# First product of a four-expert mixture by seven half-size products, with sums of its weights made once and streamed

## The chip, the cores and the metric

The kernel runs on one core of one Trainium2 chip. The metric is the device time of one execution in microseconds (us); lower is better. All arithmetic is in float32.

## The reference

Two blocks follow each other. The first is a recurrence over 768 steps for 4 x 8 heads of width 40; the second is a mixture of four two-layer networks on the 3072 x 320 rows that the first one gives.

```python
# r, k, v, w, a, b: (B=4, H=8, S=768, D=40)
for t in range(S):
    y[:, :, t] = einsum('bhd,bhde->bhe', rt, state)
    Sa = einsum('bhde,bhe->bhd', state, at)
    state = state * wt[:, :, None, :] - einsum('bhd,bhe->bhde', Sa, bt) + einsum('bhd,bhe->bhde', vt, kt)
x = y.transpose(0, 2, 1, 3).reshape(3072, 320)
p = domain_probs / (domain_probs.sum(-1, keepdims=True) + 1e-9)
for e in range(4):                      # w1: (4, 320, 1024), w2: (4, 1024, 320)
    out += p[:, e:e + 1] * (maximum(x @ w1[e], 0) @ w2[e])
```

## The kernel before

**Units and chunks.** The sequence is cut into 12 chunks of 64 steps. A unit is one chunk of two batch entries (16 heads, 128 partitions of tokens), so there are 24 units; two units of one chunk make 256 rows for the mixture. `within` prepares a unit (decays, triangular scores), `substitute` inverts small triangles (on GpSimd from unit 2 on), `merge` joins the inverses, and `step` carries the state and ends with `Y`, the unit's result. For chunks from the third on, `step` moves `Y` into the transposed rows `xT` (320 feature rows in three groups of partitions, by 256 tokens) with twelve small DMAs on SyncE's queue (line 750).

**The mixture of a chunk** (`mixture_of_chunk`). For each of the four experts: two calls of `up_main`, each for half of the 1024 hidden columns, multiply `xT` by w1, 128 x 128 weights against 256 moving columns; the last 64 of the 320 features are done by `up_last` with four 64 x 64 tiles of the array. ScalarE applies the relu into `hs`. The second product (hidden rows times w2) is already done by seven half-size products instead of eight: `add_h` makes five sums of `hs` on VectorE (`a1`, `a7`, `a5`, `a2`, `a6`), `add_weights` made the sums of w2 once, and `down_1` and `down_2` multiply and let VectorE add the results, scaled by the gate, to the output tile `osb`. The results of matmuls of the mixture share three PSUM banks, tag `mm`, taken in turn; a bank is taken again only when the readers of its former content are done.

**Order.** The matmuls are kept in program order. A list `todo` holds the pieces of the mixture, and the main loop (line 1106) puts two of them into each of four gaps between the attention stages of a unit, so an expert takes two gaps and a chunk takes the eight gaps of two units. The second product of an expert is run in the gaps of the next expert. `lead` runs the 64 x 64 part of a piece ahead of it. After the last unit the remaining pieces run back to back.

**Weights.** w1 doesn't stay on the core. `load_piece` brings half an expert (512 KB and twice 64 KB) into one of two buffers for each use, and `used` starts the load of a later piece when a buffer comes free. All these loads, the loads of the inputs, the moves into `xT` and the stores of the output stand in one queue, SyncE's (SP), whose instructions are carried out in order. VectorE and ScalarE also work their queues in order, in an order that is fixed when the program is built.

Of the kernel before, what the change touches and what calls it, by code (L numbers as in the profile page):

```python
# [15 lines left out]
def kernel(  # L16
# [184 lines left out]

    def load(q, names):
        for x in names:
            q.n[x] = t = sb.tile([P, H, D], FP32, name=f"nat{x}", tag=f"nat{x}", bufs=2 if x in "WV" else 1)
            for i, bb in enumerate(q.b):
                nc.sync.dma_start(
                    out=t[i * L:(i + 1) * L], in_=srcs[x][bb, :, q.c * L:(q.c + 1) * L, :].rearrange("h t e -> t h e"),
                )
# [52 lines left out]

    w2_sb = [const.tile([P, NF, DM], FP32, name=f"w2_{e}") for e in range(E)]
    gate = const.tile([P, NC, B // 2, E], FP32, name="gate")
    minus_gate = const.tile([P, NC, B // 2, E], FP32, name="minus_gate")
# [10 lines left out]
    class Piece:  # L277
        pass

    n_pieces = 2 * E * (1 + NC)  # L280
    pieces = []

    in_sums = {k + 5 * x: k - 1 for x in range(3) for k in (1, 2, 3)}
# [1 line left out]
    def load_piece():  # L285

        k = len(pieces)
        e, x = k // 2 % E, k % 2
        if k in in_sums:
            t = sums[in_sums[k]]  # L290
        else:
            t = sb.tile([P, PIECE], FP32, name="w1p", tag="w1p", bufs=2)
        q = Piece()
        q.main = t[:, 0:2 * HF * P].rearrange("p (g c) -> p g c", g=2)
        q.last = t[:, 2 * HF * P:PIECE].rearrange("p (f c) -> p f c", c=P)
        cols = slice(x * HF * P, (x + 1) * HF * P)
        moves = [(q.main, moe_w1[e, 0:2 * P, cols].rearrange("(g p) c -> p g c", p=P))]
        for i in range(2):
            half_cols = slice((2 * x + i) * HF // 2 * P, (2 * x + i + 1) * HF // 2 * P)
            moves.append(  # L300
                (q.last[i * DT:(i + 1) * DT], moe_w1[e, 2 * P:DM, half_cols].rearrange("d (f c) -> d f c", c=P))
            )
        for to, src in moves:
            tc.keep_in_program_order(nc.sync.dma_start(out=to, in_=src))
        pieces.append(q)

    def used(n):

        while len(pieces) < n_pieces:
            k = len(pieces)  # L310
            if k in in_sums:
                before = k - 5 if k >= 5 else -1
            else:
                at = [x for x in range(k) if x not in in_sums]
                before = at[-2] if len(at) > 1 else -1
            if before >= n:
                break
            load_piece()

    def load_w2(e):  # L320
        tc.keep_in_program_order(nc.sync.dma_start(out=w2_sb[e][:], in_=moe_w2[e].rearrange("(f p) d -> p f d", p=P)))
# [84 lines left out]
    def within(q):  # L406
# [43 lines left out]
        yield  # L450

        pg = by(turn("pg", tok(Gv), q.u == 2)[:], 64)[:, :, 0:D]
        gp = sb.tile([P, H, D], FP32, name="gp")
        pin(nc.vector.tensor_tensor(out=gp[:], in0=pg, in1=n["W"][:], op=ALU.mult))
        pin(nc.vector.reciprocal(out=gp[:], in_=gp[:]))  # L455

# [314 lines left out]
    def up_main(k, xT, n, ph):  # L771

        w1 = pieces[k]
        h = sb.tile([P, HF, 2 * P], FP32, name="hs", tag="hs", bufs=3)
        for i in range(2):
            for f in range(HF // 2):
                for g in range(2):
# [29 lines left out]
    def mixture_of_unit(q):  # L807
# [3 lines left out]
        def ups(e):  # L811
# [6 lines left out]
            def piece():  # L818
                lead()
                hs[e] = [up_main(at + 2 * e, q.xT, P, ph[0])]  # L820
                hs[e].append(up_main(at + 2 * e + 1, q.xT, P, up_last(at + 2 * e + 1, q.xT, P)))
                used(at + 2 * e + 2)
                if q.u == 0 and e + 2 < E:
                    load_w2(e + 2)

            piece.lead = lead
# [32 lines left out]
    def add_weights(e):  # L859

        b = {(q, x): of_w2(e, q, x) for q in range(2) for x in range(2)}
        for to, x, y, op in (
# [6 lines left out]
            tc.keep_in_program_order(nc.vector.tensor_tensor(out=to, in0=x, in1=y, op=op))  # L869
            yield  # L870

    def mixture_of_chunk(qs, xT):

        hs, a_sums, osb = {}, {}, []
        at = 2 * E * (qs[0].c + 1)

        def ups(e, x):
            k, ph = at + 2 * e + x, []

            def lead():  # L880
                if not ph:
                    ph.append(up_last(k, xT, 2 * P))

            def piece():
                lead()
                hs[e, x] = up_main(k, xT, 2 * P, ph[0])
                used(k + 1)

            piece.lead = lead
            return piece  # L890

        def of_h(e, s, x):
            return hs[e, x][:, :, s * P:(s + 1) * P]

        def add_h(e):
            a = {(s, x): of_h(e, s, x) for s in range(2) for x in range(2)}
            for n, x, y, op in (
                (1, a[0, 0], a[1, 1], ALU.add), (7, a[0, 1], a[1, 1], ALU.subtract),
                (5, a[0, 0], a[0, 1], ALU.add), (2, a[1, 0], a[1, 1], ALU.add),
                (6, a[1, 0], a[0, 0], ALU.subtract),  # L900
            ):
                t = a_sums[e, n] = sb.tile([P, HF, P], FP32, name=f"a{n}")
                nc.vector.tensor_tensor(out=t[:], in0=x, in1=y, op=op)  # L903

        def products(name, *terms):
            p = ps.tile([P, len(terms) * HD], FP32, name=name, tag="mm", bufs=3)
            for n, (a, b) in enumerate(terms):
                for f in range(HF):
                    matmul(
                        out=p[:, n * HD:(n + 1) * HD], lhsT=a[:, f, :], rhs=b[:, f, :],  # L910
                        start=(f == 0), stop=(f == HF - 1),
                    )
            return p

        left, right, wide = slice(0, HD), slice(HD, DM), slice(0, DM)

        def down_1(e):
            p = products(
                "p431", (of_h(e, 1, 1), of_w2(e, 1, 0)), (of_h(e, 0, 0), of_w2(e, 0, 1)),
                (a_sums[e, 1], of_sums(e, 0)),  # L920
            )
            if e == 0:
                osb.extend(outputs() for _ in qs)

            for q, o in zip(qs, osb):
                add(o[:], p[:, wide], scale(q, e), e == 0)
            for q, o, cols in zip(qs, osb, (left, right)):
                add(o[:, cols], p[:, DM:DM + HD], scale(q, e))

        def down_2(e):  # L930
            p75 = products("p75", (a_sums[e, 7], of_sums(e, 2)), (a_sums[e, 5], of_w2(e, 1, 1)))
            p26 = products("p26", (a_sums[e, 2], of_w2(e, 0, 0)), (a_sums[e, 6], of_sums(e, 1)))
            for q, o, p, cols, n in ((qs[0], osb[0], p75, left, 1), (qs[1], osb[1], p26, right, 0)):
                add(o[:], p[:], scale(q, e))
                add(o[:, cols], p[:, n * HD:(n + 1) * HD], scale(q, e, minus=True))
            if e == E - 1:
                for q, o in zip(qs, osb):
                    store(q, o)

        def down_2_at_end(e):  # L940

            p75 = products("p75", (a_sums[e, 7], of_sums(e, 2)), (a_sums[e, 5], of_w2(e, 1, 1)))
            p2 = products("p2", (a_sums[e, 2], of_w2(e, 0, 0)))
            p6 = products("p6", (a_sums[e, 6], of_sums(e, 1)))
            add(osb[0][:], p75[:], scale(qs[0], e))
            add(osb[0][:, left], p75[:, right], scale(qs[0], e, minus=True))
            store(qs[0], osb[0])
            add(osb[1][:, left], p2[:], scale(qs[1], e))
            add(osb[1][:, right], p2[:], scale(qs[1], e, minus=True))
            store(qs[1], osb[1], left)  # L950
            add(osb[1][:, right], p6[:], scale(qs[1], e))
            store(qs[1], osb[1], right, nc.scalar)


        before = last[:]
        for e in range(E):
            todo.append(ups(e, 0))
            if before:
                todo.append(before[0])
                todo.append(ups(e, 1))  # L960
                todo.append(lambda e=e, then=before[1]: (then(), add_h(e)))
            else:
                todo.append(lambda e=e, then=ups(e, 1): (then(), add_h(e)))
            second = down_2_at_end if (qs[0].end and e == E - 1) else down_2
            before = [lambda e=e: down_1(e), lambda e=e, second=second: second(e)]
        last[:] = before


# [47 lines left out]
    ws = [within(units[u]) for u in range(3)]  # L1016
    norm = normalize()
    keep_warm(16)
    run(ws[0], 1)
    go(load_raw(units[1], "W"))  # L1020
    run(ws[0], 1)
# [16 lines left out]
    substitute(units[0], nc.vector, scores_of(0))  # L1038
    run(ws[0], 1)
    set_pick()  # L1040
    m, s = merge(units[0]), begin_step(0)
    run(m, 1)
    run(ws[0])
# [4 lines left out]
    load(units[2], "W")  # L1048
    for x in "VR":
        load_padded(units[2], x)  # L1050
    load_piece()
    load_piece()
    run(ws[1], 1)
    go(load_raw(units[2], "A"))
    load_w2(0)
    load_piece()
    load_piece()
    run(m)
    run(ws[1], 1)
    run(s, 3)  # L1060
# [16 lines left out]
            run(norm)  # L1077

    substitute(units[1], nc.vector, scores_of(1), during_second)
    m, s = merge(units[1]), begin_step(1)  # L1080
    run(m, 1)
    run(ws[2], 1)
# [23 lines left out]
    for u in range(1, NU):  # L1106
# [38 lines left out]
        if u == 1:  # L1145
            mixture_of_unit(q)
        elif q.bp:
            mixture_of_chunk(units[u - 1:u + 1], chunks_x[q.c])
        if not early:
            begin_later(len(later))  # L1150
            run(w, 1)
# [85 lines left out]
```

## Time and profile before

| | |
|---|---|
| device time, median of 3 runs | 1097.55 us (1096.2 to 1104.36) |
| profiled execution: its own time | 1096.91 us |
| profiled execution: span | 1095.2 us, mean TensorE clock 0.988 |
| busy: TensorE matmul / weight load | 1068.1 us / 959.0 us |
| busy: VectorE / ScalarE / GpSimd | 759.0 / 353.4 / 490.3 us |
| DMA | 122.19 MB, mean 112 GB/s |

A row of the profile gives line, engine, operation, "out<-in", shapes and count, then the busy time, the mean length of one, and the idle time before it with what ended it. Matmuls overlap, so that the mean length of one is longer than the distance to the next; a float32 matmul leaves two records. PE is TensorE, PEld its weight loads, DVE VectorE, ACT ScalarE, POOL GpSimd, SPq the queue of SyncE.

### The profile page before, as it was taken

How to read it: one execution, taken by the hardware profiler on the slowest of the kernel's cores; microseconds unless marked ns; L12 is line 12 of the kernel's file. 1: busy time of each engine (PE TensorE's matmuls, PEld its weight loads, DVE VectorE, ACT ScalarE, POOL GpSimd, SP SyncE). 2: the span in 40 equal slices, each digit the busy share in tenths (PEclk: the TensorE clock that was granted, in tenths of full speed). 3: DMA queues.
4: the chain of work that ended last, by engine and by line, in shares of the span. 5: the costliest groups of instructions: out<-in, count | busy, mean ns of one | idle time of the engine just before them, and what ended most of it. 6: DMA issues, size and time to landing. Idle time of an engine off the chain costs nothing.

```text
span 1095.2 us, 38536 instructions
## 1 busy us (share of the span) xinstructions
PE 1068.1 (98%) x16102; PEld 959.0 (88%) x16102; DVE 759.0 (69%) x1551; ACT 353.4 (32%) x956; POOL 490.3 (45%) x1274
## 2 busy tenths in 40 slices
PE   7798999999999999999999999999999999999998
PEld 6677788889998999999999999989999999998887
DVE  7676569887776777767768768767777676544343
ACT  2432444234223333333233242343333332221110
POOL 5206577763472562653643634735625536420000
PEclk8799999999999999999999999999999999999999
DMA  7876545434444463454454454444543532322320
GB/s 118 236 231 142 131 91 131 107 77 108 120 119 105 110 144 97 103 146 97 100 133 105 106 122 106 115 99 105 131 103 85 149 89 60 99 71 79 107 75 13
DMA packets 268869, 122.19 MB, mean 112 GB/s; under 512 B 213736, under 2 KB 242072, under 8 KB 268696
## 3 DMA queue, kind: packets, MB, share of 16 engines
q1 hardware_dynamic: 265416, 119.12, 43.4%
q8 instruction: 127, 2.08, 0.8%
q10 hardware_dynamic: 3280, 0.61, 0.4%
q14 instruction: 46, 0.38, 0.1%
HBM read 111.79 MB, written 3.93 MB: 106 GB/s over the span
## 4 chain that ended last, share of the span: by engine, by line
PE 92%; DVE 4%; ACT 1%; DMA 1%; issue 1%; SPq 0%; DVEq 0%; ACTq 0%
PE ph L76 39%; PE p L76 31%; PE pdy L76 3%; PE psat L76 2%; PE pxr L76 2%; PE po L76 2%; PE prn L76 2%; PE pfe L76 1%; PE pc L76 1%; PE pQ L76 1%; PE pev L76 1%; PE pg L79 1%; PE pY L76 1%; DVE Z L595 1%; PE pe L76 1%
## 5 line engine op out<-in xcount | busy, mean ns | idle before, releaser
L76 PE MATMUL ph<-xT,w1p 128*128 128x256 f32 (+3 forms) x3040 | 443.9, 375 | 3.7 <-issue 3.6
L76 PEld LDWEIGHTS ph<-xT,w1p 64*64 64x64 f32 (+1 forms) x3040 | 337.7, 162 | 59.3 <-issue 18.9
L598 POOL TENSOR_TENSOR Z<-Z 128x31 f32<-128x31 f32 (+7 forms) x704 | 254.8, 362 | 55.2
L903 DVE TENSOR_TENSOR a<-hs 128x512 f32<-128x512 f32 x220 | 153.3, 714 | 105.9 <-ACT hs L784 105.9
L784 ACT ACTIVATE hs<-ph 128x512 f32<-128x512 f32 (+1 forms) x208 | 117.1, 564 | 332.0 <-PE ph L76 331.7
L585 POOL TENSOR_TENSOR Z<-M,Z 128x62 f32<-128x62 f32 (+7 forms) x352 | 148.6, 422 | 99.0 <-DVE M L574 73.1
L76 PE MATMUL p<-sums,a 128*128 128x160 f32 x1056 | 164.9, 299 | 0.0
L76 PEld LDWEIGHTS p<-sums,a 128*128 128x128 f32 x1056 | 152.8, 190 | 2.2
L797 DVE SCALAR_TENSOR_TENSOR osb<-p,gate,osb 128x320 f32<-128x320 f32 (+1 forms) x243 | 108.0, 481 | 62.6 <-PE p L76 57.5
L555 POOL COPY below<-F 32x256 f32<-32x256 f32 x48 | 21.4, 446 | 232.2 <-ACT F L511 230.6
L76 PEld LDWEIGHTS p<-w,hs 128*128 128x128 f32 x704 | 98.6, 190 | 8.5 <-issue 7.3
L76 PE MATMUL p<-w,hs 128*128 128x160 f32 x704 | 104.9, 302 | 0.0
L76 PE MATMUL p<-w,a 128*128 128x160 f32 x704 | 102.8, 299 | 0.0
L76 PEld LDWEIGHTS p<-w,a 128*128 128x128 f32 x704 | 98.0, 190 | 0.0
L617 POOL COPY QT<-QTc 32x256 f32<-32x256 f32 x96 | 40.4, 421 | 81.9 <-DVE QTc L611 68.7
L706 ACT COPY RS<-pxr 64x256 f32<-64x256 f32 x88 | 32.2, 366 | 99.7 <-DVE SX L404 66.6
L540 ACT COPY EV<-pev 64x160 f32<-64x160 f32 x96 | 23.0, 286 | 91.6 <-PE pev L76 91.2
L455 DVE RECIPROCAL gp<-gp 128x320 f32<-128x320 f32 x24 | 51.6, 2151 | 0.7
L404 DVE COPY_PREDICATED VC<-mask_up,pc 128x256 f32<-128x256 int32 x48 | 18.7, 442 | 45.4 <-PE pc L76 45.3
L558 DVE STREAM_TRANSPOSE M<-blocks 128x1024 f32<-128x1024 f32 x24 | 47.2, 1969 | 2.9 <-ACT blocks L552 2.4
L511 ACT COPY F<-pfe 128x256 f32<-128x256 f32 x48 | 15.5, 376 | 80.9 <-PE pfe L76 79.3
L76 PE MATMUL pdy<-VC,k_tok 64*64 64x104 f32 (+1 forms) x768 | 38.2, 259 | 0.0
(149 smaller groups left out, 1343.9 us busy)
## 6 DMA issues: line engine op xcount, KB each, us to landing
w1p<-in_moe_w_dram SPq DMA_DIRECT2D x95, 512.0 KB
w1p<-in_moe_w_dram SPq DMA_DIRECT2D x190, 64.0 KB
w<-in_moe_w_dram SPq DMA_DIRECT2D x4, 1280.0 KB
sums<-in_moe_w_dram SPq DMA_DIRECT2D x9, 512.0 KB
natW<-in_w_dram SPq DMA_DIRECT2D x48, 80.0 KB
natB<-in_b_dram SPq DMA_DIRECT2D x48, 80.0 KB
natK<-in_k_dram SPq DMA_DIRECT2D x48, 80.0 KB
out_dram<-osb SPq DMA_DIRECT2D x46, 80.0 KB
```

The lines of the kernel that those rows point to most:

```text
L76: return stated(nc.tensor.matmul(**k))
L455: pin(nc.vector.reciprocal(out=gp[:], in_=gp[:]))
L540: nc.scalar.copy(out=of_slot(q.EV[half(p)], i ^ p)[:, :, 0:D], in_=pev[i][half(p)])
L555: tc.keep_in_program_order(nc.gpsimd.tensor_copy(out=q.below[quarter(i)], in_=q.F[quarter(i), :, 0:Q]))
L558: ins = nc.vector.transpose(out=M[:], in_=cols)
L585: ins = eng.tensor_tensor(out=Z[:, 1:3, 0:n, j + 1:Q], in0=M[:, j:j + 2, None, j + 1:Q].to_broadcast([P, 2, n, m]), in1=Z[:, here, 0:n, j: ...
L598: eng.tensor_tensor(out=z[:, 0], in0=z[:, 0], in1=z[:, x], op=ALU.add)
L617: ins = nc.gpsimd.tensor_copy(out=q.QT[quarter(i), :, quarter(i % 2)], in_=QTc[quarter(i)])
L706: nc.scalar.copy(out=RS[half(s), x ^ s::2], in_=prs[x][half(s)].rearrange("p (j i) t -> p j i t", i=2),)
L784: nc.scalar.activation(out=h[:, i * HF // 2:(i + 1) * HF // 2, 0:n], in_=ph[i][:], func=ACTF.Relu,)
L797: nc.vector.scalar_tensor_tensor(out=to, in0=p, scalar=sc, in1=to, op0=ALU.mult, op1=ALU.add)
L903: nc.vector.tensor_tensor(out=t[:], in0=x, in1=y, op=op)
```

## The change

For the chunks from the third on (`FIRST = 2`), `mixture_by_seven` takes the place of `mixture_of_chunk`. The product of 256 rows, 256 features and 1024 hidden columns is cut in two in each direction, and the four results are made of seven products of 128 rows x 128 features x 512 columns instead of eight. This needs four sums of the rows (`add_x`, on VectorE once a chunk), four sums of the quarters of w1, and seven results that are joined: one product (`u`) is left standing in its PSUM bank and two more are added onto it there, ScalarE copies it out three times, and VectorE adds the other banks (`plus`, five times an expert). The relu is applied in SBUF afterwards. The last 64 features are still multiplied separately (`lasts_of`), now with 128 moving columns a matmul.

The sums of w1 are made once, on GpSimd (`sum_quarters`, 16 operations at the start), in the memory of w2, stored to DRAM (`store_quarters`, 4 MB in all) and afterwards loaded block by block. A ring of five blocks of 256 KB replaces the two pieces; seven blocks and one block of last features are loaded for each expert and chunk. The second product keeps its seven products, in another grouping (`p43`, `p175`, `p26`). `natV` has one buffer instead of two, and `gp` is written over `natW`.

```diff
+    BLOCKS = ((0, 0), (1, 0), (1, 1), 3, 1, 2, 0)
...
+    def load_blocks(upto):
+        while len(blocks_w) < min(upto, n_blocks):
+            n = len(blocks_w)
+            e, at = expert(n // len(BLOCKS)), BLOCKS[n % len(BLOCKS)]
...
+            tc.keep_in_program_order(nc.sync.dma_start(out=slot(n).rearrange("p f c -> p (f c)"), in_=src))
...
+            def piece_one():
+                lead_one()
+                x = bank("u")
+                product(k, 0, x, True)
+                nc.scalar.copy(out=hs[0, 0], in_=x[:])
+                product(k, 1, one[0])
+                plus(hs[0, 0], hs[0, 0], one[0][:])
+                relu(hs[0, 0])
+                product(k, 2, one[1])
+                product(k, 3, x)
+                nc.scalar.copy(out=hs[0, 1], in_=x[:])
+                plus(hs[0, 1], hs[0, 1], one[1][:])
+
+                def then():
+                    product(k, 4, x)
+                    nc.scalar.copy(out=hs[1, 0], in_=x[:])
+                    load_blocks(7 * k + 10)
+
+                then() if k == 0 else before[0](then)
...
+            def piece_two():
+                lead_two()
+                load_last(k + 1)
+                product(k, 5, two[0])
+                product(k, 6, two[1])
+                plus(hs[1, 1], hs[1, 0], two[1][:])
+                plus(hs[1, 0], hs[1, 0], two[0][:])
+                plus(hs[0, 1], hs[0, 1], two[1][:])
+                relu(hs[1, 0])
+                nc.scalar.activation(out=both, in_=both, func=ACTF.Relu)
+                load_blocks(7 * k + 12)
+                before[1]()
+                add_h(lambda s, x: hs[s, x], a_sums)
...
+    load_quarters(0, nc.scalar)
+    load_quarters(1, nc.scalar)
...
+    sum_quarters(0)
+    sum_quarters(1)
...
+    store_quarters(0, nc.sync)
     load_piece()
     load_piece()
+    store_quarters(1, nc.sync)
+    load_quarters(2, nc.sync)
     run(ws[1], 1)
+    sum_quarters(2)
...
-            mixture_of_chunk(units[u - 1:u + 1], chunks_x[q.c])
+            (mixture_of_chunk if q.c < FIRST else mixture_by_seven)(units[u - 1:u + 1], chunks_x[q.c])
```

In `piece_one`, `before[0](then)` runs `p43` of the expert before, and puts `then` (product 4) between its two halves.

## The prediction

> **What bounds the kernel now.** I read the page's shares first, then the chain of waits, then one pair of units in the window view, then the timelines of single engines.
>
> ```profile
> PE 1068.1 (98%) x16102; PEld 959.0 (88%) x16102; DVE 759.0 (69%) x1551; ACT 353.4 (32%) x956; POOL 490.3 (45%) x1274
> PE 92%; DVE 4%; ACT 1%; DMA 1%; issue 1%; SPq 0%; DVEq 0%; ACTq 0%
> 560.00:645.24 85.24, 85.24 (x1339) 77.95 (x1339) 63.08 (x127) 29.14 (x80) 41.74 (x110) 1.00 0.46 111
> ```
>
> The end is set by TensorE, with no gap at all in the stretch of 85.24 us that is two units. So one unit is 42.62 us, and matmul time taken out is a gain as long as PE stays the last to be ready. But the third number says that VectorE is already busy for 63.08 of the 85.24 us.
>
> ```profile
> 583.05 3.45 PE ph L76 x16
> 93.79 1.06 PE L76 MATMUL ph<-xT,sums 128*128 128x128 f32 x8
> 604.77 2.34 PE L76 MATMUL p<-w,hs 128*128 128x160 f32 x16
> 1040.14 4.75 PE L76 MATMUL ph<-xT,w1p 64*64 64x256 f32 x32
> 1057.10 4.75 PE L76 MATMUL ph<-xT,w1p 64*64 64x256 f32 x32
> ```
>
> From the chain: 16 records with 256 moving columns take 3.45 us, 216 ns each. From the timeline: eight with 128 columns take 1.06 us to the end of the last, whose own length is 0.275, so (1.06-0.275)/7 = 112 ns each. With 160 columns it is (2.34-0.30)/15 = 136 ns. The last two lines are the same step of two experts in the pure mixture at the end: 16.96 us an expert.
>
> ```profile
> 637.61 1.30 DVE L903 TENSOR_TENSOR a<-hs 128x512 f32<-128x512 f32 x2 [1.65 <-ACT hs L784]
> 639.15 0.55 DVE L797 SCALAR_TENSOR_TENSOR osb<-p,gate,osb 128x320 f32<-128x320 f32 x1 [0.25 <-PE p L76]
> 625.14 8.95 SPq L750 DMA_DIRECT2D xT<-Y  x12
> 634.99 1.79 SPq L304 DMA_DIRECT2D w1p<-in_moe_w_dram  x3
> 101.44 3.34 DMA sums<-in_moe_w_dram
> 132.99 5.04 DMA w1p<-in_moe_w_dram
> 42.42 0.86 POOL L481 TENSOR_TENSOR k_tok<-natK,gp 128x320 f32<-128x320 f32 x1 [7.47 <-issue]
> 43.24 1.52 POOL L485 TENSOR_TENSOR AT<-AT,G 128x512 f32<-128x512 f32 x1
> ```
>
> VectorE: two 512-wide sums in 1.30 us, so 0.62 a slot and 0.68 alone; a 320-wide addition from PSUM holds a slot of 0.46, a 160-wide one 0.30 (their timeline starts). SP: the twelve moves into `xT` hold its queue for 8.95 us, and a load behind them starts afterwards. The DMA pieces of the chain say that 512 KB land 3.3 to 5.0 us after the issue. GpSimd takes 1.52 us for a 512-wide operation of two inputs.
>
> **What the Trainium skill says.** "TensorE: Matmul & The Clock Gate", section "LDWEIGHTS (loading the stationary operand)", gives columns / 1.2 ns, 107 ns for 128: a 128-column matmul then streams hardly longer than its weights load. The 112 ns agree. "DMA: Bandwidth & Descriptors", section "Anatomy of one DMA — SWDGE (gpsimd) path": a DMA's semaphore wait is spent on the issuing sequencer, so everything behind it in SP's queue waits too; here `SPq L304 <- PE ph` stands at 91.4 us in the waits of SP. "Perfetto Trace Analysis", section "DMA Instruction — HWDGE (DVE, Sync)": the profiler's bar of a DMA is its issue, not the movement; here issues of w1 take about 0.5 us, landings 3.3 to 5.0.
>
> **Matmuls removed and added.** Before, an expert's first product has 16 matmuls of 256 columns: 32 records x 216 = 6.91 us. After, 7 x 4 matmuls of 128 columns: 56 x 112 = 6.27 us. The 64 x 64 part before has 32 records in 2 x 0.95 us; after, 64 records at half the columns, taken as equal. The second product keeps 56 records of 136 ns. So PE gains 0.64 us an expert, 1.28 us a unit, 25.6 us in all (40 experts), and no more: a seventh less than eight eighths would be 0.86 us, but 112 is more than half of 216.
>
> **VectorE.** Five `plus` an expert. No row has a 512-wide addition from PSUM; below, it can't beat the 533 ns of 512 elements at the slope of the 160- and 320-wide rows; above, 0.74 by extending them; I take 0.62. So 4 x 5 x 0.62 = 12.4 us, and about 1.2 for `add_x`, on 63.08: 76.7 of the 82.7 us that PE would need for two units. VectorE would be 93% busy, in order, with PE waiting for it at new places. ScalarE grows by three copies and three relus less four relus, about 1.5 us an expert on 29.14/85.24; it is covered.
>
> **One unit walked through** in the built order of each engine, with the durations above. Let T be the end of product 6 of an expert.
>
> First half (the one with `pfe`, `psat`, `pe`, `pxr`). VectorE after T: three `plus` to 1.9, but `a7` waits for the relu of 1024 columns (1.03 us by the ScalarE rows of 256 and 512) until 2.45; `a7`, `a1`, then the four additions of `p175` with `a5` and `a2` between them: to 6.35. Only then the bank of `c12` is free. PE is through `p175`, `p26` and `pfe` at 3.26+2.17+0.62 = 6.05: waits 0.35. `a6` and the `p26` additions free the bank of `u` at 8.4, when PE has done lasts and `psat`: no wait. The 3.6 us around the transpose `M` stand ahead of the next `plus`, done at 12.6; PE is ready for `p43` at 12.2: waits 0.45. Product 4 waits 0.1 for a ScalarE copy that is behind a relu that is behind that `plus`. The half ends at 20.4 instead of 19.4.
>
> Second half (`pg`, `pev`, `pdy`, then `pNT` to `pQ`). After its T, VectorE does the same sums, with 0.7 us of slowing as in the trace of before while GpSimd works, then the 2.07 us reciprocal, then `Y`: ready 12.5 after T, 32.9 in the unit. Now SP issues the twelve `xT` moves, 8.95 us: 41.85. Behind them in its queue stand blocks 5 and 6 of the expert that is being multiplied; together 512 KB, so landed at 45.2 to 46.9. Product 6 takes 0.9 more: the unit ends at 46.1 to 47.8. Without this load PE and VectorE alone would end it at 44.6: VectorE's run of reciprocal, `Y`, state and `k_tok` makes `p43` wait 1.3 us, and the decay work ahead of the next `plus` takes the rest. Before, the load behind the moves was for a piece needed much later, so it cost nothing; the ring of five blocks for seven leaves only these two without lead.
>
> I take 46.8 a unit, 4.2 more than 42.62. It applies from the first `mixture_by_seven` piece (after `pdy` of unit 5, 237 us) to about 945, where the preparation of units ends: 708/42.62 = 16.6 units, +70 us.
>
> **The end.** From 1003 on some 4.7 experts run back to back. By the same walk `c12` and `u` wait for additions: 17.3 against 16.96, +1.5 us. The stretch 945 to 1003, where VectorE has less to do, I put at 0.
>
> **The start.** Sixteen GpSimd operations of 1.52 us. Eight stand ahead of the first copy into `below`, in an idle stretch of 16.22 us, and are covered if their weights have landed by 17. Four more (6.1 us) stand ahead of the `k_tok` and `AT` operations at 42.42, and wait for a load that is in SP's queue behind 2 MB of stores and two pieces. That is 4.3 MB from 28 us on, at the 269 to 338 GB/s of the windows there 13 to 16 us, so these operations end 51 to 54 instead of 44.76, of which 3.5 us are free until `pfe`. With the 2 MB that now run beside the first input loads: +8, from +2 to +20.
>
> **Sum.** 1096.9 (own time of the profiled execution, 1.7 over its span, 0.65 under the median) + 70 + 1.5 + 8 = 1176.4; the median may be taken as the same.
>
> **Rivals.**
> - *VectorE alone is the new bound* (the two blocks come in time, because `Y` comes sooner or the moves issue faster): 44.6 a unit, 16.6 x 2.0 = 33, with the end and start 1139. For it: 63.08 us and the order above; against: the queue of SP in the trace has hardly a gap between 622 and 642.
> - *PE stays the bound, faster.* The one mechanism: VectorE runs its own preparation work early, in the 22 us it is idle per pair of units, so that no bank is late. Then 1.28 x 16.6 + 0.64 x 7 other experts = 25.6 less, start +8: 1079. It decides if `plus` on `c11` is done before PE reaches `p43`, and blocks 5 and 6 land within 1.5 us of the moves' end. Against: VectorE's order is fixed, and its idle time is waiting for data.
> - *Raw loads late too.* SP gets six more DMAs a unit (0.4 to 0.6 us each, 64 instead of 58) and the transposes of V and R stand ahead of `plus`; in the trace they waited for DMA 31.2 and 9.4 us already. 2 us more a unit: 1210.
> - *It doesn't save the matmuls it says*: the counts leave no room for that.
>
> **How the numbers follow.** Load behind the moves: 0.50, 1150 to 1195. VectorE alone: 0.28. Raw loads late: 0.12. Faster by over 1%: 0.06. Within 1%, by a mixture of gains and waits: 0.04. Slower by over 1%: the first three, 0.90. A measurement here can tell about 1% from no change. The range reaches over the first three cases with their bounds: 1122 to 1220; it leaves out the faster cases and the far end of the third.
>
> **What would show it.** Right: PE below 95% busy in the middle; a unit of 45 to 48 us; weight loads of `c21` or `c22` after the `xT` moves waiting for a DMA of `w_mem`, and `c12`, `p43` waiting for VectorE; VectorE over 80%. 128-column records 112 ns apart. Wrong: PE without gaps, and a unit of 41.3.

## The result, and the profile after

The changed kernel takes 1271.05 us (1269.84 to 1272.13) beside 1097.34 us: ratio 1.157, interval 1.152 to 1.162. The direction was right; the size was not: 174 us instead of 79.5, and above the range of 1122 to 1220.

The page after, in the order in which it was read before: shares of the engines, chain of waits, then two units in the window view, and in the last line all of units 5 to 21 (columns: window, its length, PE, PEld, DVE, ACT and POOL busy with counts, granted clock, DMA share, GB/s).

```profile
PE 1104.4 (87%) x18342; PEld 1024.5 (81%) x18342; DVE 894.1 (70%) x1801; ACT 414.2 (33%) x1036; POOL 516.0 (41%) x1290
PE 45%; DVE 23%; DMA 12%; SPq 11%; issue 5%; ACT 2%; DVEq 0%; POOL 0%; POOLq 0%
610.53:710.22 99.69, 87.17 (x1576) 82.41 (x1567) 75.56 (x153) 34.96 (x86) 43.19 (x112) 0.98 0.51 127
259.60:1064.90 805.30, 704.30 (x12426) 667.39 (x12425) 602.88 (x1210) 276.82 (x682) 335.94 (x864) 0.97 0.49 124
```

TensorE carried 92% of the chain and had no gap; now it carries 45% and stands still for 12.5 of the 99.69 us of two units. No engine took its place: VectorE is 76% busy there, SP's queue and DMA together make 23% of the chain. The bound is now a sequence of waits. Cut at the first `pdy` of units 5 and 21 (here and below, a unit runs from one first `pdy` to the next), the span divides as follows.

| us | before | after | more | forecast |
|---|---|---|---|---|
| start to unit 5 | 235.3 | 259.6 | 24.3 | 8 |
| units 5 to 21 (16 units) | 681.7 | 805.3 | 123.6 | 67 |
| the same, a unit | 42.61 | 50.33 | 7.7 | 4.2 |
| unit 21 to the end | 178.1 | 204.2 | 26.1 | 4 |

The forecast's 16.6 units are divided here into 16 and 0.6. Three waits, added up over the whole span (engine and tile, what it waited for, us in all, times, longest):

```profile
PE p L76 <- DVE h_mem L1098: 42.1, 30, 3.8
PE c L76 <- DMA w_mem<-w_sums: 37.2, 24, 5.3
DVE AT L245 <- DMA rawA<-in_a_dram: 34.4, 7, 6.0
```

TensorE waits for VectorE (`p` needs a sum that `plus` and the relu finish) and for streamed blocks. The third line was not foreseen: VectorE itself waits for a raw input. The end of one unit in the timelines of SP, PE and VectorE shows how they hang together (start, duration, then in brackets the idle time before and its releaser).

```profile
616.42 8.92 SPq L823 DMA_DIRECT2D xT<-Y  x12
625.45 1.96 SPq L379 DMA_DIRECT2D w_mem<-w_sums  x2
627.49 1.33 SPq L379 DMA_DIRECT2D w_mem<-in_moe_w_dram  x3
628.88 0.42 SPq L227 DMA_DIRECT2D rawA<-in_a_dram  x1
```

```profile
628.59 1.16 PE L76 MATMUL c<-xT,w_mem 128*128 128x128 f32 x8 [1.49 <-DMA w_mem<-w_sums]
630.65 1.16 PE L76 MATMUL c<-x_sums,w_mem 128*128 128x128 f32 x8 [0.90 <-DMA w_mem<-w_sums]
...
637.11 1.32 PE L76 MATMUL p<-w,a 128*128 128x160 f32 x8 [2.04 <-DVE h_mem L1098]
```

```profile
634.33 0.71 DVE L245 STREAM_TRANSPOSE AT<-rawA 128x512 f32<-128x512 f32 x1 [5.33 <-DMA rawA<-in_a_dram]
635.08 0.69 DVE L558 TENSOR_TENSOR AT<-AT,G 128x512 f32<-128x512 f32 x1
635.69 1.88 DVE L1098 TENSOR_TENSOR h_mem<-h_mem,c 128x512 f32<-128x512 f32 x3
```

The twelve moves hold SP until 625.34. Blocks 5 and 6 leave after them, and products 5 and 6 wait 1.49 and 0.90 us: the forecast's step. But the fourth load of raw A leaves only at 628.88, and VectorE's order has that transpose ahead of the three `plus`. VectorE idles 5.33 us with `plus` queued behind, and PE waits 2.04 us for its result. This is what stands in whose way; what each part costs is for the experiments to show.

### The profile page after: what moved, and what is told of

Its sections match the earlier page's. It is cut to its first block, busy times and chain, and to the rows that moved or that the text cites. A ratio compares the mean times of both kernels' runs of the same rounds, so it can differ in the third digit from the quotient of the medians.

```text
span 1269.1 us, 44050 instructions
## 1 busy us (share of the span) xinstructions
PE 1104.4 (87%) x18342; PEld 1024.5 (81%) x18342; DVE 894.1 (70%) x1801; ACT 414.2 (33%) x1036; POOL 516.0 (41%) x1290
## 4 chain that ended last, share of the span: by engine, by line
PE 45%; DVE 23%; DMA 12%; SPq 11%; issue 5%; ACT 2%; DVEq 0%; POOL 0%; POOLq 0%
PE p L76 15%; PE c L76 11%; PE u L76 5%; DVE a L957 4%; DVE osb L871 4%; PE ph L76 4%; SPq L227 4%; DVE h_mem L1098 3%; DVE natW L528 3%; DMA w_mem<-w_sums 3%; SPq L206 2%; SPq L823 2%; DMA w_mem<-in_moe_w_dram 2%; DMA rawA<-in_a_dram 2%; PE pxr L76 2%
## 5 line engine op out<-in xcount | busy, mean ns | idle before, releaser
L76 PE MATMUL c<-xT,w_mem 64*64 64x128 f32 (+1 forms) x3200 | 188.7, 276 | 49.1 <-DMA w_mem<-w_sums 32.1
L1098 DVE TENSOR_TENSOR h_mem<-h_mem,c 128x512 f32<-128x512 f32 x200 | 130.0, 683 | 119.4 <-PE c L76 74.8
L76 PEld LDWEIGHTS c<-xT,w_mem 64*64 64x64 f32 (+1 forms) x3200 | 159.2, 146 | 62.3 <-DMA w_mem<-w_sums 34.8
L957 DVE TENSOR_TENSOR a<-h_mem 128x512 f32<-128x512 f32 x220 | 154.2, 717 | 20.0 <-ACT h_mem L1153 15.2
L871 DVE SCALAR_TENSOR_TENSOR osb<-p,gate,osb 128x160 f32<-128x160 f32 (+1 forms) x243 | 114.2, 481 | 50.8 <-PE p L76 50.6
L76 PE MATMUL p<-w,h_mem 128*128 128x160 f32 x704 | 112.5, 304 | 25.5 <-DVE h_mem L1098 25.3
L76 PEld LDWEIGHTS p<-w,h_mem 128*128 128x128 f32 x704 | 98.1, 190 | 31.4 <-DVE h_mem L1098 30.9
L76 PEld LDWEIGHTS p<-w,a 128*128 128x128 f32 x704 | 100.6, 194 | 18.7 <-issue 16.6
L76 PE MATMUL u<-xT,w_mem 128*128 128x128 f32 x640 | 90.7, 285 | 8.2 <-issue 5.9
L76 PE MATMUL c<-x_sums,w_mem 128*128 128x128 f32 x640 | 92.2, 290 | 5.1 <-DMA w_mem<-w_sums 5.1
L76 PEld LDWEIGHTS c<-x_sums,w_mem 128*128 128x128 f32 x640 | 83.5, 204 | 7.5 <-DMA w_mem<-w_sums 6.4
```

The costliest lines, as they stand in the source:

```text
L76: return stated(nc.tensor.matmul(**k))
L871: nc.vector.scalar_tensor_tensor(out=to, in0=p, scalar=sc, in1=to, op0=ALU.mult, op1=ALU.add)
L957: eng.tensor_tensor(out=t[:], in0=x, in1=y, op=op)
L1098: nc.vector.tensor_tensor(out=to, in0=x, in1=y, op=ALU.add)
```

## Experiments

**First round: the stream off SP, and less VectorE work.** Four kernels, each with one edit.

```diff
 # e1_stream_act (load_blocks, load_last)
-nc.sync.dma_start(out=slot(n)..., in_=src)
+nc.scalar.dma_start(out=slot(n)..., in_=src)
 # e2_plus_narrow (plus)
+to, x, y = (t[:, :, 0:4] for t in (to, x, y))
 # e3_both: both edits
 # e4_start_alone
-FIRST = 2
+FIRST = NC
```

> The whole stream of w1 (blocks and lasts) is issued from ScalarE's queue instead of SP's; nothing else changes. Theory 1, the queue: a large part of the loss is loads that stand in SP's queue behind the twelve moves of xT (blocks 5 and 6, the fourth load of raw A, the lasts of the next expert). Then the weight loads' waits for w_mem go, and the raw loads come sooner because fewer DMAs stand ahead of them: a unit of about 45 us instead of 50.3 over units 5 to 21, so -5 x 16 = -80, and 1190 in all (1175 to 1215). Theory 2, VectorE: the sums alone make the unit, and a load that arrives earlier only moves the wait to VectorE: less than 1 us a unit, 1255 or more. The start and the end stay as they are in both.

Measured: 1296.91 us, 1.180 (1.178 to 1.182), slower than the change itself. Theory 1 missed; the number lies where theory 2 put it (1255 or more), but not for its reason. ScalarE's own copies now stand behind the block loads, and TensorE waits for one of them (`Yq`) 28.1 us in all, where it was 1.5 in the changed kernel:

```profile
639.44 3.55 ACTq L379 DMA_DIRECT2D w_mem<-in_moe_w_dram  x3
643.03 1.06 ACT L706 COPY Yq<-pY 32x128 f32<-32x128 f32 x4 [7.13 <-DMA natB<-in_b_dram]
PE pQ L76 <- ACT Yq L706: 28.1, 16, 4.3
```

The issues themselves are short, 0.33 to 0.37 us each (at 639.44, 641.22 and 642.63). ScalarE stands still between them, until a move into `xT` lands by the trace.

> The five additions by which an expert's half-size products are gathered (plus) are made on 4 of the 128 tokens only, so this kernel leaves out most of the work of these additions; their places, waits and banks stay. VectorE loses about 5 x 0.6 = 3 us an expert, 6 us a unit. Theory 1, the queue: blocks 5 and 6 and raw A still stand behind the moves of xT, which start when Y is ready, about 2 to 3 us sooner: a unit of 47.5 to 49, and 1235 in all (1220 to 1250). Theory 2, VectorE: the unit falls by the better part of the 6 us, to 44.5 to 46, and with 0.5 us an expert at the end the total is 1180 (1165 to 1210).

Measured: 1258.41 us, 1.148 (1.142 to 1.154), outside the ranges of both theories.

> Both at once: the stream of w1 from ScalarE's queue, and plus on 4 of 128 tokens (so most of the work of these additions is left out). If queue and VectorE are all that stands in the way in the middle and at the end, the unit comes to 42 to 43 us: 1271 - 16 x 7.8 - about 8 at the end = 1138, with the loss at the start of some 24 us left in it (1120 to 1155). If it stays above 1165, a third cause is at work in the middle (the banks of PSUM, ScalarE's relus, or the clock).

Measured: 1263.05 us, 1.150 (1.147 to 1.153). With the blocks off SP's queue and `plus` made cheap the time hardly moved, because TensorE then waited for the preparation of the next unit, as the waits of this kernel show (17.6 us in the changed kernel):

```profile
PE pY L76 <- DVE QTc L684: 49.0, 17, 5.9
```

These three kernels can't be read as single edits. The orders of the engines are drawn by the scheduler from estimated times. By the traces VectorE's order is another one in all three, and ScalarE's in e1 and e3; in e3 the addition of `add_x`, which waits for the moves, had come ahead of `QTc`. What follows from this round is that the order is part of what is measured. From here on each kernel writes out the order of VectorE, ScalarE, GpSimd and SP: that of the changed kernel, except where told.

> All chunks take the old first product, so no half-size product and no stream are left; the start keeps its loads, 16 sums on GpSimd and stores of w1's quarters, and the second product keeps the changed grouping into p43, p175 and p26. The walk of the traces puts the loss up to the first product by seven at 24 us, the prediction at 8: 1121 (1115 to 1128) against 1105. The grouping itself is taken at nothing; if it costs VectorE something (5 additions from p175 and p26 instead of the old ones), it would show as more than 0.3 us an expert in the end.

Measured: 1133.09 us, 1.031 (1.030 to 1.033), above the range given, with the sums made and stored but not used. Unit 5 is reached at 255.2 us, 19.9 later than before; units 5 to 21 take 9.2 more, 6.4 of it unit 6 alone, and the end 4.3 more. From unit 9 on a unit takes 42.60 us, before 42.50, so the new grouping of the second product costs next to nothing there. Of the 35 us, 19.9 belong to the start; the others fall later, and e4 doesn't say whether the start's work, the memory layout or the grouping causes them.

**Amount of VectorE work, at a fixed order.** The edit of e2, with the orders of the changed kernel kept.

> In the two runs with narrow additions the scheduler had redrawn the order of VectorE's and the queues' work (over a thousand lines of difference), so they say little. Here the orders of VectorE, ScalarE, GpSimd and SP are written out and are those of the changed kernel, instruction for instruction; only the five additions of an expert are made on 4 of 128 tokens (most of their work is left out). Theory VectorE: its busy time falls by about 5 us a unit and with it most of the 7.7: a unit of 45 to 46, total 1180 to 1200. Theory queue: the loads behind the moves of xT come only as much sooner as Y does (0.5 us), VectorE stands waiting for raw A: a unit of 48.5 to 49.5, total 1240 to 1255.

Measured: 1247.05 us, 1.135 (1.128 to 1.142). This lies in the range of the queue theory. The 200 `plus` keep VectorE busy for 130 us in the changed kernel, and making them nearly free gives 24. The amount is not what bounds this order.

**Order alone.** Every instruction and every byte as in the changed kernel; only the order in one queue differs (in p4 in two).

```diff
 # p2_sp_order: SP, end of a unit
-xT moves x12; blocks 5, 6; next blocks x3; raw A; natW, natB, natK, natV; last features
+blocks 5, 6; raw A; xT moves x12; next blocks x3; last features; natW, natB, natK, natV
 # p3_dve_order: VectorE, end of a unit
-transpose of raw A and its product; xT sums; plus x3
+plus x3; transpose of raw A and its product; xT sums
 # and plus on c11 directly behind the first two instructions of Y
 # p4_both_orders: both
```

> All orders as in the changed kernel, except in SP's queue from unit 7 on: blocks 5 and 6 of an expert in its second half and the load of raw A that stood behind the twelve moves of xT are put ahead of them, and the lasts of the next expert ahead of the loads of natW, natB, natK and natV. Theory queue: the weight loads' waits for w_mem (37 us of them for w_sums, 9 for the lasts) and VectorE's 34 us for raw A go: 50.3 - (1.5 + 0.9 + 2.0 and a part of the clock's loss) = 46 a unit, total 1195 (1185 to 1215). Theory VectorE: what PE waits for is then plus instead, at most 1 us a unit gained: 1255 or more.

Measured: 1223.14 us, 1.113 (1.109 to 1.117): 48 us of the 174 for the order of one queue, between the ranges of the two theories. In SP's timeline the two blocks and the last load of raw A now leave ahead of the moves, which start at 605.24:

```profile
603.80 0.87 SPq L379 DMA_DIRECT2D w_mem<-w_sums  x2
604.72 0.42 SPq L227 DMA_DIRECT2D rawA<-in_a_dram  x1
```

The waits of TensorE:

```profile
PE p L76 <- DVE h_mem L1098: 33.3, 31, 2.1
PE c L76 <- issue: 22.5, 20, 1.8
PE c L76 <- DMA w_mem<-w_sums: 4.0, 6, 1.3
```

The late blocks (37.2 us) and the late raw A (34.4, now 0.6) are nearly gone; a unit takes 47.2 us on average (units 9 to 21). PE waits for `plus` as often as in the changed kernel, never longer than 2.1 us. The middle line was 5.0 us there. The profile names no releaser for it, but in one unit PE goes on with `c` at 624.76, right after VectorE has ended the last of the four additions of `p175` at 624.66: the wait for the bank of `c12` that the forecast walked through.

> All orders as in the changed kernel, except VectorE's: in the second half of a unit the transpose of raw A and its product, and the addition that waits for the moves into xT, are put behind the three plus instead of ahead of them; and plus on c11 directly behind the two additions that make Y from pdy, ahead of state, n_tok and k_tok. No work is added or removed. Theory order: the stall for raw A no longer holds the banks and p43 waits less; without it 1.6 + 2.0 us a unit go, but blocks 5 and 6 are as late as before: 47 a unit, total 1215 (1200 to 1235). If a wait for raw A only moves to pfe, nothing is gained: 1260.

Measured: 1274.44 us, 1.161 (1.156 to 1.166): nothing. The stall has only moved. VectorE no longer waits for raw A, and PE's wait for `plus` (42.1 us) is nearly gone, but PE comes sooner to products 5 and 6 and waits there for their blocks (37.2 us in the changed kernel):

```profile
PE c L76 <- DMA w_mem<-w_sums: 70.0, 18, 7.4
PE p L76 <- DVE h_mem L1098: 2.1, 7, 0.7
```

So the late raw A alone costs nothing as long as the blocks stand behind the same moves.

> Both changed orders at once, the same work. If the loss in the middle is the order of two queues and not the amount of work on VectorE (76.7 of 82.7 us for two units by the forecast), the unit comes down to 43 to 44: total 1160 (1140 to 1175), the start's 24 and the end's part included. If VectorE's amount of work is the bound, it stays at 45 or more and the total over 1185.

Measured: 1227.52 us, 1.119 (1.114 to 1.124), no better than p2, and over the 1185 above which VectorE's amount of work was to be the bound. But the trace shows a late transfer again:

```profile
PE c L76 <- DMA w_mem<-w_sums: 26.1, 13, 3.4
```

4.0 us in p2 are 26.1 here. These waits now fall in the first half of a unit, where blocks 5 and 6 stand behind sixteen loads of raw V and R. p2 leaves them there as well.

**Fuller orders.** v2 also puts these blocks ahead of raw R, and reorders VectorE by what TensorE asks for next: the additions of `p175` directly behind `plus`, `a2` and `a6` late, `Y` and one `plus` ahead of the reciprocal, `Qc` and `QTc` ahead of the additions of `p43`. `w1_dve_order_only` has v2's VectorE order with the SP order of the changed kernel. `v2_narrow` adds the edit of e2 to v2.

> The same work as the changed kernel in other written-out orders, on top of the run with SP's changed order. SP: in the first half of a unit too, blocks 5 and 6 ahead of the eight loads of raw R. VectorE: the four additions from p175 directly behind the three plus (their bank is that of c12), a2 and a6 behind plus on c12, Y ahead of the reciprocal of natW, plus on c11 ahead of the reciprocal, Qc and QTc ahead of the additions from p43, the transpose of raw A behind the plus. Nothing is added or left out. Theory order: the waits of PE for plus, for banks, for QTc and for blocks, 5 us a unit in that run, fall to about 1 us: a unit of 42.5 to 43.5, total 1140 (1125 to 1160). Theory VectorE's amount: it has 38 us of work a unit and idles for data in places that no order moves; then the unit stays at 45 or more, total over 1185.

Measured: 1168.02 us, 1.065 (1.061 to 1.068). The same work, 103 us faster than the change as it was; it lies between the ranges of the two theories.

```profile
573.85:661.29 87.44, 84.42 (x1575) 80.85 (x1567) 78.26 (x153) 35.08 (x86) 43.43 (x111) 1.00 0.56 144
PE p L76 <- DVE h_mem L1098: 12.9, 24, 1.1
```

These two units take 87.44 us, 43.7 each, beside 99.69 and beside 85.24 before (44.1 on average in units 9 to 21); VectorE is busy for nearly the same time (78.26 to 75.56) and therefore 90% busy. PE's wait for `plus` fell from 42.1 to 12.9 us, and its wait for the additions of `p175` (22.5 in p2) to 0.4.

> VectorE's order of the fuller run (additions from p175 first, Y ahead of the reciprocal, a2 and a6 late, raw A behind plus), with SP's order as in the changed kernel. If the two orders are two separate losses, this one takes away its own part: 1271 less 55 = 1215. If SP's late loads are the first thing that ends a wait in every unit, VectorE's order alone is worth little, as with the smaller reordering (1274): 1255 to 1275.

Measured: 1232.12 us, 1.122 (1.120 to 1.124): VectorE's order alone gives 39 us and SP's alone 48 (p2's version of it); together 103, more than the sum of 87. That a late transfer also stalls VectorE may be why, but v2 moves more blocks than p2, and no run has v2's SP order alone.

> The same orders, and the five plus of an expert on 4 of 128 tokens (most of their work is left out). Theory order: little is left for it to gain: 0.5 to 1 us a unit, 1125 (1110 to 1140). Theory VectorE's amount: 3 us a unit and more, 50 us and more in all.

Measured: 1157.69 us, 1.054 (1.051 to 1.057). With good orders, nearly all the work of `plus` is worth 10 us.

**The start.** On e4, with its own orders written out: first the sums on 4 of 512 columns, then also the loads and stores of the quarters on 8 of 128 rows.

```diff
 # s1_start_no_sums (sum_quarters)
-nc.gpsimd.tensor_tensor(out=to, in0=x, in1=y, op=ALU.subtract)
+nc.gpsimd.tensor_tensor(out=to[:, 0:4], in0=x[:, 0:4], in1=y[:, 0:4], op=ALU.subtract)
 # s2_start_no_bytes: besides, in load_quarters and store_quarters
-quarters(e)[:, g]
+quarters(e)[0:8, g]
```

> From the run in which all chunks take the old first product (1133 against 1098): all orders kept, the sixteen sums of w1's quarters on GpSimd made on 4 of 512 columns (most of their work is left out); their loads and stores stay. If GpSimd's 16 x 1.5 us ahead of the copies into below and ahead of k_tok are the start's loss, 20 of the 35 us go: 1113. If the loss is the 8.4 MB of loads and stores in the first 100 us, which the sums only wait for, under 8 us go: 1127.

Measured: 1126.74 us, 1.026 (1.023 to 1.030): 6.4 less than e4, of it 2.5 before unit 5. This agrees with the theory of the bytes.

> As the run before it, and the loads of w1's quarters and the stores of the sums move 8 of 128 rows (a sixteenth of the bytes); the same instructions in the same order. What is left over the kernel before is the layout, the grouping into p43, p175 and p26 and the places of the issues in SP's queue: taken at 5 us, so 1104 (1100 to 1112). The difference to the run before it is the price of the bytes.

Measured: 1116.32 us, 1.017 (1.014 to 1.020): 10.4 less again; unit 5 comes at 240.1 instead of 252.7. So 12.6 of e4's 19.9 us belong to the bytes, 2.5 to the sums, and 4.8 remain. Up to unit 4 s2 is only 1.0 us behind the kernel before, the changed kernel 19.2. The timelines of SP and of GpSimd in the changed kernel show one path by which this reaches the units:

```profile
41.62 1.04 SPq L350 DMA_DIRECT2D w_sums<-w  x2
43.18 2.23 SPq L335 DMA_DIRECT2D w<-in_moe_w_dram  x2
```

```profile
50.19 1.27 POOL L346 TENSOR_TENSOR w<-w 128x512 f32<-128x512 f32 x1 [7.57 <-DMA w<-in_moe_w_dram]
...
56.49 0.94 POOL L554 TENSOR_TENSOR k_tok<-natK,natW 128x320 f32<-128x320 f32 x1
```

The load of the third expert's quarters stands in SP behind the stores of the first two, GpSimd waits 7.57 us for it, and `k_tok` stands behind these sums: 56.49 us, before 42.42. Without sums and bytes it starts at 42.89 (s2). A second path is earlier: in the chain of the changed kernel the first `natK` takes 8.77 us to land, and ScalarE's first copy to `F` starts at 20.80 us instead of 14.46; in s2 it starts at 14.99.

> The fuller orders of SP and VectorE (1168), and the start's work moved, none of it left out: ScalarE issues the first four loads of w1's quarters behind its copy of KT instead of ahead of it, GpSimd makes the first eight sums behind the two copies into below, the next four behind k_tok and AT, the last four behind the next two copies into below. If the start's loss is where this work stands, the first pdy of unit 5 comes at 242 instead of 257: total 1153 (1148 to 1160). If it is the bytes that the memory has to move in that time, it stays within 5 us: 1163 or more.

Measured: 1171.24 us, 1.067 (1.065 to 1.069): v2 with the quarter loads issued later and the sums behind the preparation work. Nothing gained, unit 5 again at 259.0. But this kernel doesn't separate place and bytes, for the quarter loads now hold ScalarE's copy to `F`, here beside the line of the kernel before:

```profile
13.94 6.14 ACTq L335 DMA_DIRECT2D w<-in_moe_w_dram  x3
20.13 0.65 ACT L584 COPY F<-pfe 128x256 f32<-128x256 f32 x2 [5.95 <-DMA w<-in_moe_w_dram]
```

```profile
14.46 0.65 ACT L511 COPY F<-pfe 128x256 f32<-128x256 f32 x2 [0.31 <-PE pfe L76]
```

So the first delay came back by another way. `k_tok`, with no sum ahead of it, still starts at 52.27. That the bytes (4 MB loaded and 4 MB stored in the first 100 us) cost most of the start rests on s2 alone.

**Once more the stream on ScalarE, at fixed places.** w2 with the blocks issued from ScalarE where their slots are already free, and a few VectorE places adjusted.

```diff
-nc.sync.dma_start(out=slot(n)..., in_=src)
+(nc.sync if n < 5 else nc.scalar).dma_start(out=slot(n)..., in_=src)
```

> As the run before it, and the blocks of w1 are issued from ScalarE at places where their slots are already free (blocks 5 and 6 behind the copy of product 3, the next three ahead of the relu of 1024 columns, the last two behind the next relu), which takes 7 DMAs an expert out of SP's queue; on VectorE plus on c11 directly behind Y, a5 behind plus on c11, the transpose of raw V behind a2 and a6. No work is left out. Theory: SP's queue is what makes raw V and raw R and some blocks late in the unit of 43.9: 42.3 to 42.8 a unit, 25 us less than the run before it: 1130 (1120 to 1142). If ScalarE's issues delay its copies, as in the first run with the stream on ScalarE, it is no faster than the run before it.

Measured: 1161.08 us, 1.057 (1.054 to 1.060), the fastest version of the change with all its work; none beat the kernel before. It missed the 1120 to 1142 that was expected. The window of two units, and the first line of TensorE's own waits:

```profile
577.17:663.23 86.06, 84.20 (x1574) 80.66 (x1566) 77.98 (x152) 35.14 (x86) 43.77 (x111) 1.00 0.62 147
PE pY L76 <- DVE QTc L684: 14.2, 17, 5.2
```

A unit of this window takes 43.0 us with VectorE 91% busy; TensorE's largest wait is now for VectorE's preparation work. With 10 us between v3 and w2, and several places changed at once, the share of the stream's queue isn't isolated.

## Why the prediction was right or wrong

**Matmul time.** The 112 ns a record stood: eight 128-column records take 1.06 us in the PE timeline of the changed kernel, as before (1.16 in the lines shown, where a wait ends just ahead of them). The prediction set the 112 beside a figure for loading weights; a weight load is a bar of 190 ns in the trace before, and the bars overlap, so what agrees is the distance of records, not the length of a load. The gain was put at 1.28 us a unit; the least disturbed unit of v3, 41.85 us long with 41.44 of PE busy, against 42.4 to 42.6 before, allows about 1.0. (What the prediction calls "a seventh less" is an eighth: 6.91 / 8 = 0.86.)

**VectorE's amount.** Right: 76.7 us for two units were forecast, and 75.56 (after) to 78.26 (v2) measured; three `plus` in a row take 1.88 us, so 0.6 a slot for the 0.62 taken, and all 200 are 130 us, 0.65 each. That VectorE would be over 80% busy failed in the changed kernel, because it waits itself, and held in v2 and v3.

**The unit walk, 46.8.** This term failed by most: it was put at 4.2 us a unit and measured 7.7, which makes 57 of the 94 us that the forecast lacks. The mechanism was right as far as it went: blocks 5 and 6 behind the moves, products 5 and 6 waiting, `c12` and `p43` waiting for VectorE. But the walk has 5.5 us of waits a unit (46.8 less 42.62, and the 1.28 gained), and 9.0 came. The last line of the window view above and TensorE's waits in units 5 to 21 divide them.

- TensorE idle: 101.0 us, 6.3 a unit. Of these 2.5 are for `plus`, where the walk has 0.45 and 1.3; 1.9 for blocks 5 and 6, about what the walk has (46.8 against 44.6 without them); 0.6 for other loads of the stream and 0.7 for `QTc`, both put at nothing.
- The clock, put at nothing. Its mean over these units is 0.972, where it was 1.000 before; as an estimate (1-0.972) x 50.3 = 1.4 us of a unit are lost to it. No run changed the clock alone.
- The remaining 1.3 us lie in time that the profile counts as busy, and are not attributed.

`plus` is later than in the walk because the walk stopped at the two blocks. Behind the same twelve moves stand raw A, whose transpose is ahead of `plus` on VectorE, and the loads after it. I followed the moves into PE's weight loads and not into VectorE's inputs. The rival "raw loads late too", 2 us a unit at 0.12, saw part of this. It would be too much to call raw A the larger cost: p3 takes its hold off `plus` and gains nothing, p2 moves blocks and raw A together, and no run moves one of them alone. And "PE and VectorE alone would end it at 44.6" was too good for the built order: with SP mended (p2) a unit takes 47.2, with VectorE mended too (v2) 44.1. So 44.6 describes orders that could be written, not those that were built.

**The stretch 945 to 1003 at nothing, the end +1.5.** The first of these failed. Units 21 and 22 take 14.9 us more, though "VectorE has less to do" there: TensorE waits 12.4 us in them where it had no wait before, 6.9 of it for `QTc`, and the clock is 0.96. The experts after them take 11.1 more. Back to back an expert takes 17.82 us, where it took 16.96 before and 17.3 was forecast; the mechanism (`c12` and `u` wait for additions) was right, and 4.7 x 0.86 = 4 of the 11.1 are this. The rest is in the main one wait of 5.29 us at 1175.80, once more for a block behind twelve moves, and the half clock after it: 0.92 over the 43 us from 1160 to 1203, as an estimate 3.4 us (the three overlap in part). The walk of the end had left these last moves out.

**The start, +8.** Measured 24.3, outside the 2 to 20 given. The working had `k_tok` and `AT` end at 51 to 54; they end at 58.75, and nothing of the delay was absorbed afterwards. Runs e4, s1 and s2 put 12.6 us on the bytes and 2.5 on the sums, so the term to be sized was what 8 MB of additional traffic do to the loads of the inputs beside it, not GpSimd's operations. Another 4 to 5 us appear in unit 4, in e4 and s2 (3.8 each) as in the changed kernel (5.1), and are not explained.

**Where the 174 us are.** With orders written by hand the change costs 71 instead of 174, so 103 us (ratios 1.157 and 1.065) are order in two in-order queues, the clock that is lost by waits included. In v2, unit 5 comes 22 us later than before, units 5 to 21 take 33 more, and the end 13 more. Of the 33, 12.4 fall in units 5 and 6 alone, where the first `mixture_by_seven` starts and the new orders only begin (SP's at 291 us, VectorE's at 305). Open remains unit 6, which takes 6.4 us more than before in e4 and 6.8 in s2: in s2 TensorE stands still once for 4.46 us in the middle of `ph`, with no releaser in the profile, and the clock is 0.93. Unit 21 of v2 has an excess of about 7 us, of it one wait of 4.2 for `QTc`.

## What to carry to other kernels

When a change puts more loads into a queue that is worked in order, follow every DMA that stands behind a late wait there to its reader, and what is queued behind that reader on its own engine: here an input of the preparation work was late behind the same moves as the new stream. To mend one of two such waits may gain nothing (p3). A busy share of 76% with waits was here a sign that order, not amount, was the cost; test it by moving instructions with all work kept, before making work cheaper. And an experiment on a kernel whose order is drawn by a scheduler needs that order pinned, or it measures another kernel.

## What the hardware showed that was not expected

Half clock after short waits. The trace lists when the granted clock changes. In the changed kernel, between 300 and 1000 us, all changes lie on a fixed grid of 3.413 us, and nine of its steps are at half clock. The window view of one such step, and of the step ahead of it with the wait of 2.04 us shown above; then a step with much of another wait, of 2.69 us from 527.47 on (the number after the five engines is the granted clock):

```profile
635.01:638.42 3.41, 1.37 (x11) 1.34 (x11) 2.85 (x6) 1.42 (x2) 0.00 (x0) 1.00 0.81 167
638.42:641.84 3.42, 3.42 (x43) 2.78 (x41) 3.42 (x8) 0.37 (x2) 0.00 (x0) 0.50 0.63 178
525.79:529.20 3.41, 1.68 (x70) 1.54 (x59) 2.83 (x8) 2.17 (x8) 0.40 (x1) 1.00 0.51 163
```

The clock is halved for 3.41 us, although TensorE is working again. The Trainium skill, "TensorE: Matmul & The Clock Gate", section "Part 1: The HAM clock gate (the "warmup" mystery)", gives half clock after at least one idle window of about 3.4 us. The length of the slow stretch agrees; the condition doesn't: TensorE was busy for 1.37 us of the step ahead of it. In all nine cases it had been idle for 1.69 to 3.21 us of that step; in the 187 steps of full clock that were followed by full clock, for 1.80 at most. In p3 the same count gives 2.01 and more against 1.97 at most. So about half a step of idle time was enough, and it counts how a wait lies on the grid: the longer wait of 2.69 us is divided into 1.73 and 0.96 by a boundary and was not followed by half clock.

DMA issues on ScalarE. In v3 the two block loads of a pair are issued in 0.33 us each, but sometimes lie far apart: at 627.33 and 630.51, and at 640.08 and 642.30. By the trace the second one goes when another DMA has landed (a move into `xT`, a load of `natW`), and ScalarE does nothing in between. In w2 the fourth quarter load waits in the same way, from 15.57 to 19.75 us, for a landing of one of the first. What ties an issue to these landings isn't shown. So moving a stream to another queue moved waits into that queue.
